# Attention and gated feed-forward on one core: the first load of k in four parts on two queues, and two one-row loads on a third

## The chip, the core and the metric

The kernel runs on one core of a Trainium2 chip. The metric is the device time in microseconds (us) of one execution; lower is better. The engines are named as in the profile: PE (TensorE, matrix products; PEld its weight loads), DVE (VectorE), ACT (ScalarE), POOL (GpSimd) and SP (SyncE, which here only issues transfers). Transfers between HBM and the on-chip memory are issued by SP, ACT or POOL, each on a queue of its own (q1, q10 and q0 in the profile), and are carried out by 16 DMA engines that all queues share.

## What is computed

Linear attention with cosine weights, then a gated feed-forward layer. Eight batches of eight heads, 576 tokens, head dimension 64.

```python
def _attn_ref(q, k, v):
    ...
    q_p = phi(q, cos_w, sin_w)          # relu(q) * cos, relu(q) * sin: 64 -> 128 features
    k_p = phi(k, cos_w, sin_w)
    kv = np.einsum('bhsf,bhsd->bhfd', k_p, v)
    z = np.sum(k_p, axis=2)
    num = np.einsum('bhsf,bhfd->bhsd', q_p, kv)
    den = np.einsum('bhsf,bhf->bhs', q_p, z)[..., None] + 1e-06
    return (num / den)
...
    rms = np.sqrt(np.mean(x * x, axis=-1, keepdims=True) + 1e-06)
    xn = x / rms * rms_g
    g = xn @ w_gate
    silu = g * (1.0 / (1.0 + np.exp(-g)))
    return (silu * (xn @ w_val) @ w_out)
```

The attention output of all heads side by side is x: 4608 tokens of 512. The feed-forward matrices are 512 x 1536 (two) and 1536 x 512. Inputs and output are float32.

## The kernel before

**The steady part.** The tokens are worked through in nine blocks of 512 (one for each batch, and one, block 8, of the last 64 tokens of the batches). In each block PE runs the gate and value products (half_mm, L556) in 12 steps, ACT and DVE turn their results into hT (L570, L571), and PE multiplies by the output matrix (out_mm, L574) in four more steps. Beside that, in slots written out by hand (the `at(block, step, where, ...)` calls), the attention of the next batch is prepared: loads, features of k and q (k_phi and q_phi, L292 on ACT and L294 on DVE), products of k and v (L387, L394), normalization (x_sq with a power on POOL at L520, x_norm at L527) and transposes through SP's queue (L346, L540).

**The beginning.** Batch 0 has no earlier block to hide behind, so its order is written out by hand. The loads are issued first:

- ACT's queue: the 2 KB vector rms_g (g4, L148). Ahead of it in ACT's program stands a table load (L62); behind it the activation that makes the table of sines and cosines, tab (L257), and then all of ACT's work on k.
- SP's queue: k of batch 0 in two loads (L150). In the tile for k, each of the 128 partitions holds nine consecutive tokens of one half of the heads: four head pairs, nine tokens, 64 values. The first load brings tokens 0 to 3 of every partition (512 KB in 512 pieces of 1 KB), the second tokens 4 to 8 (640 KB in 512 pieces of 1.25 KB).
- POOL's queue: half of q of batch 0 (load_q0, L135), v of batch 0 in two loads that convert it to bf16 (vv0, L213), the other half of q, then the feed-forward weights and the loads of batch 1 (L183, L110).

While they are under way PE runs ten matmuls on zeros (filler, L598). Then, for each token c of nine, `k_phi(V, 0, c, 0)` on DVE and `k_phi(A, 0, c, 1)` on ACT (the last one on DVE too) make the features, and z0_pe (L410) adds them up on PE; for c below 4, PE also spreads rms_g (g_spread, L233). k_phi of a token reads all four head pairs. Next kv0_pe (L430) multiplies features and v, two head pairs at a time; q's features are made and turned (q_tr_pe, L363), the sums are put in place (z0_turn, L421), kv0_pe does the other head pairs, and the chain through nd0_pe, x_sq, x_norm and x_tr_pe gives the first tokens of x, from which the dense feed-forward work of block 0 starts (unit_mm, L643).

**The late loads.** From batch 3 on (`wide`), load_kv lays k and v out with five consecutive tokens in a partition, and 576 tokens fill 115 partitions and a fifth of one more. For batch 7, the last of all, there is no next batch whose rows could fill that partition up, so a third load (L119) writes it: the last token, repeated five times, 40 pieces of 256 bytes. It is issued once for k, in step 0 of block 5, and once for v, in step 3 of block 5, by SP as all loads of load_kv at that point are. The tiles of the loads are a ring of five (`raw`).

Of the kernel before, what the change touches and what calls it, by code (L numbers as in the profile page):

```python
# [17 lines left out]
def kernel(  # L18
# [11 lines left out]
    nc = tc.nc  # L30
    B, H, S, D = q.shape
# [4 lines left out]
    HP = H // 2  # L36
    NC = S // 64
# [9 lines left out]
    V, A, G = nc.vector, nc.scalar, nc.gpsimd  # L47
# [22 lines left out]
    def kv_rows(src, b, hps):  # L70
        return src[b, 2 * hps[0] : 2 * hps[1], :, :].rearrange(
            "(hp hh) (s c) d -> (hh s) hp (c d)", hh=2, c=NC
        )

    def wide(b):
        return b > 2
# [4 lines left out]
    def kv_rows5(src, b, r0, r1):  # L81
        part = src[b, :, 0 : NC5 * (KP - 1), :].rearrange(
            "h (p c) d -> p h (c d)", c=NC5
        )[r0 : min(r1, KP - 1)]
        return bass.AP(part.tensor, part.offset, [[NC5 * D, r1 - r0]] + list(part.ap)[1:])
# [6 lines left out]
    def raw_tile(which, b):  # L92
        if (which, b) not in raw:
            t = ring.tile([P, H * NC5 * D], FP32, name="raw", tag="raw")
            raw[(which, b)] = t
        return raw[(which, b)]

    def raw_kv(which, b):
        t = raw_tile(which, b)
        if wide(b):  # L100
            return t[:, :].rearrange("p (h e) -> p h e", h=H)
        return t[:, 0 : HP * NC * D].rearrange("p (hp e) -> p hp e", hp=HP)
# [4 lines left out]
    def load_kv(which, b, hps=(0, HP), eng=nc.sync):  # L107
        src = k if which == "k" else v
        if not wide(b):
            return eng.dma_start(  # L110
                out=raw_kv(which, b)[:, hps[0] : hps[1], :], in_=kv_rows(src, b, hps)
            )
        last = KP if b < B - 1 else KP - 1
        for r0, r1 in ((0, KM), (KM, last)):
            eng.dma_start(
                out=raw_kv(which, b)[r0:r1, :, :], in_=kv_rows5(src, b, r0, r1)
            )
        if last < KP:
            eng.dma_start(  # L119
                out=raw_kv(which, b)[last:KP, :, :].rearrange("p h (c d) -> p h c d", d=D),  # L120
                in_=src[b, :, S - 1 : S, :].rearrange("h s d -> s h d").unsqueeze(2)
                .to_broadcast([1, H, NC5, D]),
            )
# [22 lines left out]

    g4 = one.tile([4, P], FP32, name="g4")
    nc.scalar.dma_start(out=g4[:, :], in_=moe_rms_g.rearrange("(t p) -> t p", p=P))  # L148
    for c0, c1 in ((0, 4), (4, NC)):
        nc.sync.dma_start(  # L150
            out=raw_kv("k", 0)[:, :, c0 * D : c1 * D],
            in_=kv_rows(k, 0, (0, HP))[:, :, c0 * D : c1 * D],
        )


# [67 lines left out]
    for i in range(3):  # L223
        m, e = math.frexp(left)
        part.append(math.ldexp(round(m * 256), e - 8))
        left -= part[i]
        G.memset(eps_rows[32 * i : 32 * i + 32, :], part[i] / 32)
    load_kv("k", 1, eng=G)
    load_w(wg, moe_w_gate, 8, NNT)

    def g_spread(bank, t):
# [12 lines left out]
        out=th[:, 0:NTAB], in0=fidx[:, :], scalar1=S - 1.0, scalar2=ang,  # L244
        op0=ALU.min, op1=ALU.mult,
    )
    for c0, c1, i0, less in ((0, 9, 0, 576.0), (13, 14, 13, 64.0), (19, NTAB, 13, 64.0)):
        V.tensor_scalar(
            out=th[64:128, c0:c1], in0=fidx[64:128, i0 : i0 + c1 - c0],
# [4 lines left out]
        out=th[:, NTAB : 2 * NTAB], in0=th[:, 0:NTAB], scalar1=math.pi / 2.0,  # L254
# [4 lines left out]
        out=sel[:, :, :], in_=ident[0:4, 0:4].unsqueeze(2).to_broadcast([4, NDT, P])  # L259
# [437 lines left out]
    x_sq(0, 1)  # L697
    load_q(1, eng=G)
    load_kv("v", 1, eng=G)
    x_norm(0, 0, (0, HALF))  # L700
    x_norm(0, 0, (HALF, DM))
# [63 lines left out]
    for j in range(4):  # L765
# [3 lines left out]
        if j < 2:  # L769
            at(0, 10 + j, "pe", q_tr_pe, 1, j, bank)  # L770
            at(0, 10 + j, "pre", q_tr_evac, V, 1, j, bank)
    at(0, 8, "post", load_kv, "k", 2, (0, HP), G)
    at(0, 9, "post", v_cast, G, 1, (0, 2))
    at(0, 10, "pre", v_cast, V, 1, (2, 4))
# [184 lines left out]
```

## Time and profile before

| what | value |
| --- | --- |
| median of 3 runs | 323.27 us (323.22 to 323.35) |
| the profiled execution | 322.91 us |
| its span, first to last instruction | 321.1 us |
| PE busy | 313.6 us (98% of the span) |
| DVE, ACT, POOL busy | 185.4, 165.8, 40.5 us |
| issue of the two k loads on SP | 0.72 to 1.73 us |
| issue of rms_g on ACT | 0.75 to 1.31 us |
| first step on k, ACT and DVE | 5.04 and 5.06 us |
| first v load: issue on POOL, down | 3.02, 9.83 us |
| kv0_pe starts | 9.87 us |
| dense work of block 0 starts (L643) | 17.3 us |
| L119 on SP (k, v) | at 195.02 for 0.80 us, at 201.80 for 1.00 us |

The span is what the profile covers; the execution's own time is 1.8 us longer. Times within the profile count from the span's start. A line such as `9.87 0.71 PE psG L430 x36` in the chain of waits means: from 9.87 us on, 0.71 us of the chain were 36 matmuls of line 430 that write psG. In the timeline the bracket at the end of a line gives the idle time of that engine just before, and what ended it. In a table of windows each engine has its busy time and, in brackets, its number of instructions; the last three columns are the granted PE clock (1.00 is full), the mean share of the 16 DMA engines that was busy, and GB/s. That share adds up the times of packets and can pass 1.

### The profile page before, as it was taken

Reading aid. Unit: us, or ns where it says so; the run is one execution under the profiler, and the core shown is the slowest. Engines: PE = TensorE matmul, PEld = TensorE weight load, DVE = VectorE, ACT = ScalarE, POOL = GpSimd, SP = SyncE. Lnnn points to the kernel's source line nnn. Section 1 sums busy time; section 2 is a strip of 40 time slices with the busy share of each in tenths; the row PEclk is TensorE's granted clock in tenths of the full one; section 3 lists DMA queues with packets and bytes.
Section 4 is the critical chain, followed back from the end, with each engine's and each line's share of the span. In section 5 each row is a group of like instructions: output and inputs, shape, how many; then the busy total and the mean of one; then the engine's idle time right before and its main releaser. Section 6 shows DMA issues by size and latency. Waiting matters only on the chain.

```text
span 321.1 us, 6023 instructions
## 1 busy us (share of the span) xinstructions
PE 313.6 (98%) x2274; PEld 162.4 (51%) x2310; DVE 185.4 (58%) x382; ACT 165.8 (52%) x322; POOL 40.5 (13%) x79
## 2 busy tenths in 40 slices
PE   7999999999999999999999999999999999999996
PEld 2689564544454445444544445544544444444444
DVE  7976977668457773777457644781676034204410
ACT  5766756754574466554744575446543233223321
POOL 9771211002001100010001100100011000000000
PEclk9999999999999999999999999999999999999999
DMA  7999999788999999999799959995522500041002
GB/s 232 239 270 269 282 329 227 201 183 190 223 226 211 187 263 187 221 247 182 162 186 230 197 163 200 197 217 163 99 59 41 116 33 0 0 102 31 1 35 98
DMA packets 80092, 53.76 MB, mean 167 GB/s; under 512 B 52235, under 2 KB 74047, under 8 KB 80063
## 3 DMA queue, kind: packets, MB, share of 16 engines
q1 hardware_dynamic: 73110, 41.25, 62.1%
q0 software_dynamic: 6944, 12.13, 15.5%
q8 instruction: 18, 0.29, 0.4%
q14 instruction: 12, 0.09, 0.1%
q10 hardware_dynamic: 8, 0.00, 0.0%
HBM read 37.83 MB, written 9.44 MB: 147 GB/s over the span
## 4 chain that ended last, share of the span: by engine, by line
PE 94%; DMA 2%; DVE 1%; issue 1%; POOL 1%; ACT 0%; POOLq 0%; ACTq 0%
PE psC L574 27%; PE psV L556 27%; PE psG L556 26%; PE psV L643 2%; PE psA L449 2%; DMA vv<-in_v_dram 2%; PE psG L574 2%; PE psG L643 2%; PE psA L387 2%; PE psA L394 1%; PE psA L474 0%; PE psV L363 0%; PE psG L430 0%; PE psC L546 0%; POOL raw L135 0%
## 5 line engine op out<-in xcount | busy, mean ns | idle before, releaser
L571 DVE TENSOR_TENSOR hT<-psV,sg 128x512 bf16<-128x512 f32 x99 | 68.2, 689 | 96.5 <-PE psV L556 64.1
L556 PE MATMUL psV<-xnT,wv 128*128 128x512 bf16 x344 | 89.6, 379 | 0.7 <-issue 0.2
L570 ACT ACTIVATE sg<-psG 128x512 f32<-128x512 f32 x99 | 58.6, 592 | 60.8 <-PE psG L556 52.7
L556 PE MATMUL psG<-xnT,wg 128*128 128x512 bf16 x337 | 88.5, 379 | 0.7 <-issue 0.2
L574 PE MATMUL psC<-wo,hT 128*128 128x512 bf16 (+1 forms) x400 | 88.4, 376 | 0.4
L574 PEld LDWEIGHTS <-hT 128*128 128x128 bf16 x456 | 43.1, 98 | 47.7
L556 PEld LDWEIGHTS <-wv 128*128 128x128 bf16 x400 | 39.0, 98 | 46.8
L556 PEld LDWEIGHTS <-wg 128*128 128x128 bf16 x400 | 37.0, 98 | 39.9 <-DVE xnT L288 0.2
L520 POOL TENSOR_TENSOR rs<-ms,mhalf 128x1 f32<-128x1 f32 x36 | 20.5, 570 | 193.9 <-ACT scr L515 193.7
L286 ACT COPY osb<-psC 128x512 f32<-128x512 f32 x32 | 18.7, 585 | 49.9 <-PE psC L574 46.1
L515 ACT ACTIVATE scr<-xt 128x513 bf16<-128x513 f32 x36 | 22.8, 635 | 23.3 <-DVE xt L499 22.3
L527 DVE SCALAR_TENSOR_TENSOR xn<-xt,rs,gb 128x512 bf16<-128x512 f32 (+1 forms) x37 | 26.9, 730 | 9.9 <-POOL rs L520 9.9
L292 ACT ACTIVATE kp<-raw,tab 128x256 bf16<-128x256 f32 (+2 forms) x51 | 28.8, 607 | 2.4 <-DMA raw<-in_k_dram 2.4
L499 DVE TENSOR_TENSOR xt<-psA,rec 128x512 f32<-128x512 f32 x36 | 24.9, 691 | 1.2
L292 ACT ACTIVATE qp<-raw,tab 128x512 bf16<-128x512 f32 (+1 forms) x36 | 23.3, 666 | 1.2 <-DMA raw<-in_q_dram 1.1
L294 DVE TENSOR_SCALAR kp<-raw,tab 128x256 bf16<-128x256 f32 (+2 forms) x53 | 20.1, 428 | 0.5 <-DMA raw<-in_k_dram 0.5
L294 DVE TENSOR_SCALAR qp<-raw,tab 128x512 bf16<-128x512 f32 (+1 forms) x34 | 15.3, 463 | 4.7 <-DMA raw<-in_q_dram 4.7
L449 PEld LDWEIGHTS <-qpT 128*128 128x128 bf16 x224 | 10.6, 97 | 6.6
L556 PE MATMUL psV<-xnT_tail,wv 128*128 128x512 bf16 x48 | 12.3, 379 | 0.1
L556 PE MATMUL psG<-xnT_tail,wg 128*128 128x512 bf16 x46 | 12.0, 379 | 0.1
L288 DVE CAST vv<-raw 116x1280 bf16<-116x1280 f32 (+1 forms) x13 | 11.1, 857 | 1.3 <-DMA raw<-in_v_dram 1.3
L449 PE MATMUL psA<-kvzs,qpT 128*128 128x65 bf16 x224 | 11.4, 193 | 0.0
(102 smaller groups left out, 177.7 us busy)
## 6 DMA issues: line engine op xcount, KB each, us to landing
out_dram<-osb SPq DMA_DIRECT2D x27, 256.0 KB, 2.3
raw<-in_q_dram SPq DMA_DIRECT2D x6, 1024.0 KB, 9.1
raw<-in_k_dram SPq DMA_DIRECT2D x5, 1120.0 KB, 8.8
raw<-in_v_dram SPq DMA_DIRECT2D x5, 1120.0 KB, 9.4
raw<-in_k_dram POOLq DMA_DIRECT2D x2, 1152.0 KB, 19.2
raw<-in_v_dram POOLq DMA_DIRECT2D x2, 1152.0 KB, 15.7
out_dram<-osb SPq DMA_DIRECT2D x17, 128.0 KB, 2.6
wg<-in_moe_w_gate_dram POOLq DMA_DIRECT2D x3, 512.0 KB, 13.8
```

Source lines behind the costliest of these rows:

```text
L286: A.copy(out=o, in_=i)
L292: A.activation(out=out_ap, in_=in_ap, func=AF.Relu, scale=scale)
L294: eng.tensor_scalar(out=out_ap, in0=in_ap, scalar1=scale, scalar2=0.0, op0=ALU.mult, op1=ALU.max)
L449: nc.tensor.matmul(heads[:, g, hp, :], lhsT=qpT[:, h, j * P : (j + 1) * P], rhs=kvzs[b][:, g, hp * E : (hp + 1) * E], start=True, stop=True,)
L499: V.tensor_tensor(out=xt[:, 0:DM].rearrange("p (hp g d) -> p g hp d", g=2, d=D), in0=heads[:, :, :, 0:D], in1=rec[:, :, :].unsqueeze(3).to ...
L515: A.activation(out=scr[:, :], in_=xt[:, 0 : DM + 1], func=AF.Square, scale=1.0 / math.sqrt(DM), accum_out=ms[:, :],)
L520: G.tensor_tensor(out=rs[:, :], in0=ms[:, :], in1=mhalf[:, :], op=ALU.pow)
L527: V.scalar_tensor_tensor(out=xn_of[(b, j)][:, c], in0=x_of[(b, j)][:, c], scalar=rs_of[(b, j)][:, :], in1=gb[:, c], op0=ALU.mult, op1=ALU. ...
L556: nc.tensor.matmul(bank[:, cols[0] : cols[1]], lhsT=w[:, t, n * P : (n + 1) * P], rhs=x[:, t, cols[0] : cols[1]], start=(t == 0), stop=(t ...
L570: A.activation(out=sg[:, :], in_=g[:, 0:TB], func=AF.Silu)
L571: V.tensor_tensor(out=hT[:, n, :], in0=v[:, 0:TB], in1=sg[:, :], op=ALU.mult)
L574: nc.tensor.matmul(bank[:, 0 : cols[1] - cols[0]], lhsT=hT[:, n, j * P : (j + 1) * P], rhs=wo[:, n, cols[0] : cols[1]], start=(n == 0), st ...
```

## The change

k of batch 0 comes in four loads in place of two, each of 256 pieces: the first four tokens of every partition in two loads on SP's queue (head pairs 0 and 1, then 2 and 3), the other five tokens in two loads on ACT's queue, split in the same way. ACT issues its two right behind rms_g. And the one-row load of L119 is always issued by GpSimd, whatever queue load_kv was given; in this program it occurs twice, for k and v of batch 7.

```diff
@@ -116,7 +116,7 @@
                 out=raw_kv(which, b)[r0:r1, :, :], in_=kv_rows5(src, b, r0, r1)
             )
         if last < KP:
-            eng.dma_start(
+            G.dma_start(
                 out=raw_kv(which, b)[last:KP, :, :].rearrange("p h (c d) -> p h c d", d=D),
                 in_=src[b, :, S - 1 : S, :].rearrange("h s d -> s h d").unsqueeze(2)
                 .to_broadcast([1, H, NC5, D]),
@@ -146,10 +146,13 @@
 
     g4 = one.tile([4, P], FP32, name="g4")
     nc.scalar.dma_start(out=g4[:, :], in_=moe_rms_g.rearrange("(t p) -> t p", p=P))
-    for c0, c1 in ((0, 4), (4, NC)):
-        nc.sync.dma_start(
-            out=raw_kv("k", 0)[:, :, c0 * D : c1 * D],
-            in_=kv_rows(k, 0, (0, HP))[:, :, c0 * D : c1 * D],
+    for eng, hps, c0, c1 in (
+        (nc.sync, (0, 2), 0, 4), (nc.sync, (2, HP), 0, 4),
+        (nc.scalar, (0, 2), 4, NC), (nc.scalar, (2, HP), 4, NC),
+    ):
+        eng.dma_start(
+            out=raw_kv("k", 0)[:, hps[0] : hps[1], c0 * D : c1 * D],
+            in_=kv_rows(k, 0, hps)[:, :, c0 * D : c1 * D],
         )
```

## The prediction, made before the changed kernel was run

> **What bounds the kernel now.** I read the page first, then PE's busy time by stages, then the chain of waits of the first 35 us, then the timeline of the first 10 us, and last the traffic of the DMA queues in small windows.
>
> ```profile
> span 321.1 us, 6023 instructions
> ```
>
> ```profile
> 0.00:17.46 17.46, 14.75 (x197) 8.42 (x200) 14.63 (x42) 12.01 (x27) 14.40 (x38) 1.00 1.01 233
> 17.46:60.00 42.54, 42.23 (x470) 28.74 (x474) 33.48 (x72) 28.56 (x58) 10.07 (x15) 1.00 1.13 278
> ...
> 190.00:222.00 32.00, 31.79 (x208) 15.68 (x211) 19.55 (x39) 16.98 (x33) 2.19 (x4) 1.00 1.02 195
> ```
>
> The first column after the length of a window is PE's busy time. From 17.46 us on PE is busy for all but about 1% of each window (42.23 of 42.54, 31.79 of 32.00). So nothing after 17.46 us can be won by an earlier transfer; an edit matters only if it moves the moment at which that dense stretch begins, and then it moves the end by as much. The change touches the first 7 us and two small loads near 195 and 202 us.
>
> The chain of waits says what sets the start of the dense stretch:
>
> ```profile
> 2.01 1.01 POOL raw L135
> 3.02 6.81 DMA vv<-in_v_dram
> 9.82 0.04 issue
> 9.87 0.71 PE psG L430 x36
> ```
>
> It is not k but v: kv0_pe (L430) waits for the first v load on GpSimd's queue, down at 9.83. k comes close behind, as the timeline shows:
>
> ```profile
> 0.72 1.01 SPq L150 DMA_DIRECT2D raw<-in_k_dram  x2
> 0.75 0.56 ACTq L148 DMA_DIRECT2D g<-in_moe_rms_g_dram  x1
> 2.43 0.24 ACT L257 ACTIVATE tab<-th 128x40 f32<-128x40 f32 x1 [0.43 <-DVE th L253]
> 5.06 3.79 DVE L294 TENSOR_SCALAR kp<-raw,tab 128x256 bf16<-128x256 f32 x10 [0.55 <-DMA raw<-in_k_dram]
> 8.91 0.39 PE L410 MATMUL psV<-kp,ones 64*128 64x512 bf16 x1
> ```
>
> The first tokens of k are down at 5.04; DVE and ACT work through k without a pause, and PE's sums of k (L410) end at 8.91 + 0.39 = 9.30. Then PE idles 0.57 until v. **The slack of k is thus about 0.53 us**: a k that is later by less costs nothing, and an earlier k alone gains nothing.
>
> **The change, part by part.** All sums are against the profiled execution (322.91 us; span 321.1, 1.8 around it); the median of the runs shown, 323.27, lies 0.36 above, and I give results on that scale.
>
> *Issues.* SP still issues two loads (0.46 and 0.49 us in the trace, 1.01 together); only their size falls. ACT gets two more behind g's, at 1.31 (0.75 + 0.56). At 0.5 to 0.56 each, by the rows above, ACT's sequencer is free again at about 2.35. What is queued behind them is the table activation at 2.43, which waits for DVE until 2.40, so it is hidden; were it 0.5 late, nobody would notice, since ACT and DVE use the table first at 5.04. Cover: 2.4 us. The first DVE and ACT instructions on k now wait for two loads in place of one: 0 to 0.06 us (the gap between SP's two issues), taken as 0.05, inside the slack.
>
> *The tiny loads.* L119 leaves SP (0.80 and 1.00 us of issue there, at 195.0 and 201.8) and goes to POOL, where the nearest rows are 0.73 to 1.08 us per issue. POOL's instruction in that stretch is the power at L520, 0.55 us each; POOL stands idle 15.55 us before the one at 199.85 and 3.83 before the one at 204.23, so 2 x 1 us fits. Were the cover gone, 1 us on POOL would delay the normalization of a token group used only from 222 us on. Their data are wanted by DVE at 213.4 (k) and 214.6 (v); POOL's loads land 6.6 to 20.9 us after issue, so k's, issued near 195, would at the slow end be down near 216. But those 20 us are 1 MB loads in the opening traffic; these carry 10 KB each. SP's transposes behind them come up to 1.8 us earlier, which PE, busy 31.79 of 32.00, cannot use. I take 0, with a bound of 0 to +0.3.
>
> *The transfers themselves.* This is the disputed part: where do the bytes of the two ACT loads come in the 16 engines' order? What the trace shows of their traffic, in windows (last two columns: share of the 16 engines, GB/s):
>
> ```profile
> 1.75:2.25 0.50, 0.50 (x3) 0.15 (x1) 0.43 (x5) 0.25 (x1) 0.50 (x7) 1.00 0.65 72
> 2.25:2.75 0.50, 0.50 (x2) 0.15 (x1) 0.50 (x3) 0.24 (x1) 0.50 (x1) 1.00 0.55 111
> 2.75:3.25 0.50, 0.50 (x2) 0.15 (x1) 0.47 (x2) 0.00 (x0) 0.50 (x2) 1.00 0.87 246
> 3.25:3.75 0.50, 0.50 (x3) 0.19 (x2) 0.47 (x2) 0.00 (x0) 0.50 (x2) 1.00 1.07 379
> ```
>
> Two things: k begins at about 1.8, some 1.1 after SP's issue, and crawls for 1.4 us before it flows at 380 to 390 GB/s. And how two queues share is seen where both have work, here k (q1) against GpSimd's queue (q0) from 5.75 to 6.25, and a transpose (q1) behind a v load (q0) from 48.7 to 49.0:
>
> ```profile
> q0 software_dynamic: 38, 0.16, 91.6%
> q1 hardware_dynamic: 33, 0.03, 19.9%
> ```
>
> ```profile
> q1 hardware_dynamic: 153, 0.04, 57.0%
> q0 software_dynamic: 18, 0.06, 49.4%
> ```
>
> The second fence is the telling one: 153 packets of one queue beside 18 of the other, although q0 had been alone until 48.5 and the transpose had been issued at 45.88. Packet about, the counts would be near equal. It looks as if each engine ends what one queue has handed it and then takes the other. By that, the ACT loads, whose first packets come at about 1.31 + 1.1 = 2.4, stand behind SP's (from 1.8) and ahead of GpSimd's (its first 7 packets fall between 5.25 and 5.75): the same order of bytes as now. First tokens 5.04 + 0.05, the others at 6.74 (L150's second issue at 1.24 plus the 5.5 us that it took to land), v at 9.83. **Sum: 0.05 inside a slack of 0.53, so 0; 323.3 us.**
>
> The Trainium skill's page "DMA: Bandwidth & Descriptors", section "Queues, rings and completion order", says otherwise: an engine goes round its queues and changes at each packet. The 153 against 18 speaks against it, but those were two different kinds of queue; by that rule the result is the first rival.
>
> **The rivals.**
>
> *First tokens late (slower).* SP's and ACT's queues alternate packet by packet from 2.4 on. The bytes moved by then: 0.5 x 72 + 0.15 x 111 = 53 KB; 471 of the 524 KB of the first tokens remain, and with 1,024 of each 2,304 bytes they need 1,060 KB of traffic. 39 + 123 KB pass until 3.25, the remaining 898 KB at 385 GB/s take 2.33: 5.58. The same sum for now (309 KB after 3.25) gives 4.05, so the first tokens are 1.5 late. That exceeds the slack of 0.53 by 1.0: PE's sums end at 10.8 in place of 9.30, and kv0_pe starts 1.0 later. 324.3. It decides from a delay of 0.53 on; with half the alternation (0.75 late) it costs 0.2. For it: engines stand 35 to 45% idle in the crawl, just when ACT's packets arrive, and an idle engine will take them. Against: the 153 to 18.
>
> *The crawl is filled (faster).* If ACT's queue uses the idle share from 2.4 to 3.25, up to 385 x 0.85 - 39 - 123 = 165 KB move earlier, 0.43 us; k ends 0.43 earlier, and since q0 set in near 5.5 only as q1 ran out, v would be down at 9.40 and kv0_pe starts 0.43 sooner. 322.8; PE's own end at 9.30 bounds the gain at 0.57. For it: the idle share. Against: the crawl is seen with the descriptors of two loads already issued, so more issues may not lift it. The Trainium skill's page "Perfetto Trace Analysis", section "DMA Optimizations", advises splitting where engines are idle; that is this rival, and the trace has the idle share only until 3.25.
>
> *The other tokens late (slower).* GpSimd's queue gets in ahead of ACT's second load. Its first q load (512 KB, 1.4 us at 385) then delays the tokens that DVE needs at 6.76; less the slack, +0.9: 324.2. Against: q0's first packets come near 5.5, three us after ACT's.
>
> **How the numbers follow.** A measurement here tells about 0.2% (0.65 us) from no change. Order kept 0.48 (323.1 to 323.5); first tokens late 0.27 (323.4 to 324.4, about two thirds of it beyond 323.9); crawl filled 0.18 (322.7 to 323.1; only if k's first tokens also gain does it pass 322.6); others late 0.07 (324.2). Slower by over 0.2%: 0.18 + 0.05 = 0.23; faster 0.07 (a third of the filled crawl); the rest, 0.70, within. The range leaves out the far end of each rival: 322.7 to 324.3.
>
> **What would show it.** Right: in the chain DMA of v still ends near 9.8, DVE's first step on k starts within 0.5 of 5.06, PE's idle before L430 stays 0.3 to 0.6. First rival: DVE's first k step after 5.6, and L430 no longer released by v but by k's features. Second: GB/s above 111 in 2.25 to 2.75 and v down before 9.6. Third: a pause of DVE and ACT in mid k. The tiny loads: any PE gap above 0.1 us between 190 and 250 us that is not there now would prove me wrong on them.

## The result, and the profile after

The changed kernel took 324.07 us (median of 22 executions, 322.88 to 326.29), the kernel before 323.26 us beside it (22 executions, 322.79 to 324.15): 1.0034 times as long, 95% interval 1.0018 to 1.005. It is slower, by 0.8 us in the median. The forecast was 323.3 us and no change that can be measured; the time lies in the range (322.7 to 324.3), but there is a change clear of the noise. The ratios here and below leave out executions more than 1.5% slower than the fastest of their kernel: one of the kernel before (414.29 us, beside e9 to e12), one of e11 (1890.86 us) and two of e14 (328.24 and 328.34 us).

The spread says more than the median: 11 of the 22 executions are slower than the slowest of the kernel before, and the other 11 have a median of 323.47. So there are two things to explain: a small loss, which the better half shows too, and a larger one that half of the executions have. The profiled execution (323.37 us) is one of the better half.

The first line of its page:

```profile
span 321.6 us, 6068 instructions
```

The timeline of the profile after, first 10 us (start, length, engine, line, operation, then the idle time and what ended it). It answers to the timeline shown of before, three lines further down in the code (L294 there is L297 here, L410 is L413, L430 is L433):

```profile
1.35 0.93 ACTq L153 DMA_DIRECT2D raw<-in_k_dram  x2
...
2.43 0.24 ACT L260 ACTIVATE tab<-th 128x40 f32<-128x40 f32 x1 [0.42 <-DVE th L256]
...
5.22 1.70 ACT L295 ACTIVATE kp<-raw,tab 128x256 bf16<-128x256 f32 x4 [2.56 <-DMA raw<-in_k_dram]
5.24 1.63 DVE L297 TENSOR_SCALAR kp<-raw,tab 128x256 bf16<-128x256 f32 x4 [0.68 <-DMA raw<-in_k_dram]
7.88 1.71 ACT L295 ACTIVATE kp<-raw,tab 128x256 bf16<-128x256 f32 x4 [0.96 <-DMA raw<-in_k_dram]
7.90 1.96 DVE L297 TENSOR_SCALAR kp<-raw,tab 128x256 bf16<-128x256 f32 x6 [1.02 <-DMA raw<-in_k_dram]
```

The first features start 0.18 later than before (5.24 for 5.06). Then both engines stop after four tokens and wait 1 us for the other five: this pause in mid k is not in the kernel before, where DVE goes through all ten steps from 5.06 to 8.85.

The chain of waits of the profile after:

```profile
1.25 3.87 DMA raw<-in_k_dram
...
5.22 0.52 ACT kp L295
...
9.64 0.37 PE psC L413
...
10.04 0.24 PE psC L413
...
10.30 0.53 PE psG L433 x36
...
17.48 0.22 PE psG L601
17.69 0.90 PE psG L646 x16
```

The load of v, which stood in the chain of before up to 9.82, is gone from it: v is down at 9.84 as before, but k's sums on PE now end after it, and kv0_pe (L433) starts at 10.12 where it started at 9.87. The first long run of dense work, at 17.46 before, comes at 17.69. From there on PE has no gap over 0.13 us, so these 0.23 us reach the end whole; the two profiled executions differ by 0.46, the rest being within what repeated runs of one kernel differ by.

How late k is, is not to be read from the time at which most of it is there. The trace has, for each load, when each of the 16 DMA engines reported its part done; an instruction that reads the load waits for the last of the sixteen (ACT and DVE go on at 7.88 and 7.90 us, just behind the 7.80 of the last). Median engine and last engine, in us:

| load of k | before | after |
| --- | --- | --- |
| first four tokens, last of their loads | 4.51, 4.95 | 4.66, 5.11 |
| other five tokens, last of their loads | 6.31, 6.74 | 6.07, **7.80** |

Fifteen engines have the last load done by 6.53, earlier than before. The sixteenth takes 1.27 us more. What it does meanwhile, in the traffic of the DMA queues of the profile after from 6.60 to 7.60 (queue: packets, MB, share of 16 engines):

```profile
q0 software_dynamic: 126, 0.26, 99.3%
q10 hardware_dynamic: 8, 0.01, 2.7%
```

The last eight packets of ACT's queue (q10) run beside GpSimd's work (q0). The trace does not name a packet's engine, but each engine ends its part of a load with a packet of 4 bytes (36 on ACT's queue: four for rms_g, sixteen for each load of k), and of the last load's sixteen fifteen have started by 6.066 and one starts at 7.265: the pieces between are the sixteenth's. Single pieces of 1,280 bytes start at 6.035, 6.242, 6.467, 6.679 and 6.916, some 0.21 us apart, though a piece takes 0.06: between two of them fits one packet of 4 KB of GpSimd's queue (0.16 to 0.22 us each in that stretch). The last six pieces, from 6.916 on, follow each other 0.05 to 0.07 us apart. So on this engine the two queues take turns packet by packet for a while. By these rows that is about half of its 1.27 us (an estimate: four spaces of 0.16 us beyond a piece's own 0.06); by the rest it was behind already. The profile of e16 below shows the turns one by one.

### The profile page after: what moved, and what is told of

Its sections match the earlier page's. It is cut to its first block, busy times and chain, and to the rows that moved or that the text cites. A ratio compares the mean times of both kernels' runs of the same rounds, so it can differ in the third digit from the quotient of the medians.

```text
span 321.6 us, 6068 instructions
## 1 busy us (share of the span) xinstructions
PE 317.2 (99%) x2310; PEld 162.7 (51%) x2310; DVE 185.1 (58%) x382; ACT 165.9 (52%) x322; POOL 41.9 (13%) x81
## 4 chain that ended last, share of the span: by engine, by line
PE 94%; DMA 3%; ACT 1%; SPq 0%; DVE 0%; issue 0%; POOL 0%; ACTq 0%
PE psG L559 27%; PE psV L559 27%; PE psC L577 26%; PE psV L646 2%; PE psA L452 2%; PE psG L577 2%; PE psG L646 2%; PE psA L390 2%; DMA xnT_tail<-xn 1%; DMA raw<-in_k_dram 1%; PE psC L413 1%; PE psA L397 1%; ACT qp L295 0%; PE psA L477 0%; PE psV L366 0%; PE psC L549 0%
## 5 line engine op out<-in xcount | busy, mean ns | idle before, releaser
L559 PE MATMUL psG<-xnT,wg 128*128 128x512 bf16 x352 | 90.3, 379 | 0.0
L297 DVE TENSOR_SCALAR kp<-raw,tab 128x256 bf16<-128x256 f32 (+2 forms) x53 | 19.9, 423 | 1.7 <-DMA raw<-in_k_dram 1.7
L297 DVE TENSOR_SCALAR qp<-raw,tab 128x512 bf16<-128x512 f32 (+1 forms) x34 | 15.2, 460 | 4.2 <-DMA raw<-in_q_dram 4.2
```

Of the source, the lines that this page charges most:

```text
L297: eng.tensor_scalar(out=out_ap, in0=in_ap, scalar1=scale, scalar2=0.0, op0=ALU.mult, op1=ALU.max)
L559: nc.tensor.matmul(bank[:, cols[0] : cols[1]], lhsT=w[:, t, n * P : (n + 1) * P], rhs=x[:, t, cols[0] : cols[1]], start=(t == 0), stop=(t ...
```

## The experiments

Two causes of a late k were open (the one-row loads, the loads of k), and for the loads of k which property of the four: a second queue (theory A), their smaller size (256 pieces in place of 512, each piece as long as before; theory C, and in narrower forms D, E and G), or their number (theory H). Theory B is that the one-row loads cost the time. Letters in the quoted expectations are those of the theories as they stood at the time; where one needs a word it is given. The ratios are to the kernel before, run beside each experiment.

### Which half of the change

**e1: the four loads alone.** The changed kernel, with the one-row load back on the queue it had:

```diff
         if last < KP:
-            G.dma_start(
+            eng.dma_start(
```

> The four loads of k as in the change; the one-row loads stay on SP. Theory A (the last tokens of k come late because their tail on ACT's queue takes turns with GpSimd's packets): as the changed kernel, 323.9 to 324.5 us, single executions up to 326, the second half of k's features starting near 7.9 us. Theory B (the one-row loads on GpSimd's queue cost the time, by disturbing PE late): as before, 323.3 us.

324.41 us (323.35 to 326.66, 12 executions), ratio 1.0043 [1.0024, 1.0062]. The whole loss is there without the one-row loads. In its profile (325.19 us) the last load of k is down on the median engine at 6.12 and on the last at 7.99, and DVE pauses for 1.26 us.

**e2: the one-row loads alone.** The kernel before with only the other edit:

```diff
         if last < KP:
-            eng.dma_start(
+            G.dma_start(
```

> Only the one-row loads move to GpSimd's queue; k of batch 0 as before. Theory A: 323.2 to 323.4 us, no execution above 324.5. Theory B: 324 us, single executions up to 326.

323.28 us (322.89 to 323.69), ratio 1.0003 [0.9995, 1.0012]: nothing. In its windows PE is busy without a break where the issues were moved:

```profile
190.00:256.00 66.00, 66.00 (x445) 32.34 (x444) 36.87 (x74) 33.44 (x66) 4.94 (x9) 1.00 0.67 138
```

Theory B falls.

### Second queue, size of a load, or number of loads

**e4: two loads as before, the second on ACT's queue.**

```diff
-    for c0, c1 in ((0, 4), (4, NC)):
-        nc.sync.dma_start(
+    for eng, c0, c1 in ((nc.sync, 0, 4), (nc.scalar, 4, NC)):
+        eng.dma_start(
```

> k in two loads of 512 pieces as before, the first on SP's queue and the second on ACT's; one-row loads on SP. Theory A: as the changed kernel, 323.9 to 324.5 us, the second half of k's features starting near 7.5 to 8 us. Theory C: 323.3 us.

322.88 us (322.49 to 324.05, 12 executions), ratio 1.0002 [0.9991, 1.0014]. The second load's parts come in between 6.01 and 6.48, no engine late, and ACT, in its timeline, goes through all its tokens at one go:

```profile
4.79 3.42 ACT L293 ACTIVATE kp<-raw,tab 128x256 bf16<-128x256 f32 x8 [2.13 <-DMA raw<-in_k_dram]
```

A second queue by itself is harmless, with GpSimd's beside it too. Theory A, which I held until then, falls.

**e3: the four loads all on SP's queue.**

```diff
-        (nc.scalar, (0, 2), 4, NC), (nc.scalar, (2, HP), 4, NC),
+        (nc.sync, (0, 2), 4, NC), (nc.sync, (2, HP), 4, NC),
```

(the one-row load as before, here and in e5, e6, e9 and e10).

> k in the same four loads of 256 pieces, all four on SP's queue; one-row loads on SP. Theory A (the second queue is what hurts): 323.2 to 323.5 us, the second half of k's features starting near 6.8 us. Theory C (the smaller loads hurt by themselves): 324 us or more, features late as in the changed kernel.

327.43 us (326.3 to 329.18, 6 executions), ratio 1.0138 [1.0116, 1.016]: the worst of all, on one queue. Its first tokens are down early, at 4.27, but the parts of the third load come in from 4.84 to 8.63 and those of the fourth from 5.74 to 9.48, and DVE waits for them, as its timeline says:

```profile
4.40 1.68 DVE L297 TENSOR_SCALAR kp<-raw,tab 128x256 bf16<-128x256 f32 x4
9.58 1.79 DVE L297 TENSOR_SCALAR kp<-raw,tab 128x256 bf16<-128x256 f32 x6 [3.50 <-DMA raw<-in_k_dram]
```

Here many engines fall behind, not one. So the queue of ACT isn't the cause; if anything it softens it.

**e5: three loads, ACT's in one.** **e6: three loads, SP's in one.**

```diff
-        (nc.scalar, (0, 2), 4, NC), (nc.scalar, (2, HP), 4, NC),
+        (nc.scalar, (0, HP), 4, NC),
```

```diff
-        (nc.sync, (0, 2), 0, 4), (nc.sync, (2, HP), 0, 4),
+        (nc.sync, (0, HP), 0, 4),
```

> First tokens in two loads of 256 pieces on SP's queue, the others in one load of 512 on ACT's; one-row loads on SP. Theory D (it is the last load's small size that lets an engine fall behind: between ACT's two small loads it turns to GpSimd's queue and then takes turns with it): the other tokens land within 6.7 us on all engines, clock at 0.999 or more in all executions, 322.6 to 323.4 us, first tokens earlier than before (under 4.9 us). Theory E (small loads at the head of SP's queue are what spreads the engines): the last engine lands after 7.3 us and 324 us or more.

> First tokens in one load of 512 pieces on SP's queue, the others in two of 256 on ACT's; one-row loads on SP. Theory D: the last engine lands at 7.3 us or later, 323.9 to 324.6 us, single executions up to 326 with a mean clock of 0.989 to 0.995. Theory E: all engines within 6.7 us and 322.8 to 323.4 us.

e5: 323.60 us (12 executions), 1.0014 [1.0002, 1.0025]; e6: 323.81 us (11 executions), 1.0012 [1.0003, 1.002]. The last load is down at 6.26 and 6.72 on the last engine, so neither of the profiled executions has the late one. What is left is about a third of the loss. Theory D asked for a late engine in e6, theory E for one in e5, and the times of both missed what either had given for the even case: neither holds as it stood.

**e9: two loads of 256 pieces** (of 2,304 bytes: all nine tokens of two head pairs), on SP. **e10: four loads of 512 pieces** (512 bytes three times, 768 once: tokens 0 and 1, 2 and 3, 4 and 5, 6 to 8), on SP and ACT. The features' first tokens need both loads in e9 and only one in e10.

```diff
-        (nc.sync, (0, 2), 0, 4), (nc.sync, (2, HP), 0, 4),
-        (nc.scalar, (0, 2), 4, NC), (nc.scalar, (2, HP), 4, NC),
+        (nc.sync, (0, 2), 0, NC), (nc.sync, (2, HP), 0, NC),
```

```diff
-        (nc.sync, (0, 2), 0, 4), (nc.sync, (2, HP), 0, 4),
-        (nc.scalar, (0, 2), 4, NC), (nc.scalar, (2, HP), 4, NC),
+        (nc.sync, (0, HP), 0, 2), (nc.sync, (0, HP), 2, 4),
+        (nc.scalar, (0, HP), 4, 6), (nc.scalar, (0, HP), 6, NC),
```

> k in only two loads, each of 256 pieces of 2304 bytes (head pairs 0 and 1, then 2 and 3, all nine tokens), both on SP's queue; one-row loads on SP. All of k's features wait for both, so the time says little; the landings decide. Theory G (an engine falls behind when its share of a load is small, 16 pieces): the last engine lands 0.8 us or more after the median engine. Theory H (it is the number of loads under way, four against two): the 16 engines land within 0.6 us of each other, by about 6.7 us, as in the kernel before.

> k in four loads of 512 pieces each (all head pairs; tokens 0-1 and 2-3 on SP's queue, 4-5 and 6-8 on ACT's, pieces of 512 to 768 bytes); one-row loads on SP. Theory G: no engine falls behind, all within 0.6 us of the median, 323.2 to 323.7 us. Theory H: the last engine lands 0.8 us or more after the median in the last load, 324 us or more, some executions with a mean clock under 0.997.

e9: its parts come in from 3.88 to 4.31 and from 5.44 to 5.81, all within 0.4 us, and all of k is down 0.9 us earlier than in the kernel before. (It is slower all the same, 325.1 us, 1.0082 [1.0054, 1.0109]: no token can start before 5.81, and in its profile the first sum starts at 6.48 and full clock is granted only at 13.70. What that has to do with each other is the last question below.) e10: 326.19 us, 1.0071 [1.0031, 1.0111]; the last load is down on the median engine at 6.58, on the last three at 8.15, 9.27 and 9.77. Its DVE and ACT, in the timeline:

```profile
9.80 1.27 DVE L297 TENSOR_SCALAR kp<-raw,tab 128x256 bf16<-128x256 f32 x4 [3.46 <-DMA raw<-in_k_dram]
...
9.80 0.91 ACT L295 ACTIVATE kp<-raw,tab 128x256 bf16<-128x256 f32 x2 [3.11 <-DMA raw<-in_k_dram]
```

So neither the number of pieces in a load nor their size decides: 256 pieces in two loads are even, 512 in four are not. Nor does the number of pieces in all, which is 1,024 in the kernel before and in the changed one. Put in one table, the last load of k in the profiled executions:

| loads of k | run | median engine, us | last engine, us |
| --- | --- | --- | --- |
| 2 on SP | before | 6.31 | 6.74 |
| 2 on SP, by head pairs | e9 | 5.67 | 5.81 |
| 1 on SP, 1 on ACT | e4 | 6.21 | 6.48 |
| 3 | e5, e6 | 6.10, 6.35 | 6.26, 6.72 |
| 4 on SP and ACT | after, e1 | 6.07, 6.12 | 7.80, 7.99 |
| 4 on SP and ACT, again | e12, e16 (below) | 6.17, 6.21 | 6.41, 10.09 |
| 4 on SP and ACT, of 512 | e10 | 6.58 | 9.77 |
| 4 on SP | e3 | 7.81 | 9.48 |

With two queues the median engine stays between 6.06 and 6.58, whatever the number of loads. The last one does not. One profile says little, since the engine is not late each time; but over all profiles, those below included, it is more than 1 us behind the median in seven of ten with four loads (after, e1, e3, e7, e10, e14, e16; 0.25 to 0.86 in e8, e11 and e12), and never more than 0.5 in six with two (before, e2, e4, e9, e13, e15). Theory H, the number of loads under way, is what is left; that small loads as such do not do it rests on e9's one profile. Why an engine falls behind when four are under way, no run shows.

### GpSimd's packets and the late engine

**e8: GpSimd's loads 0.85 us later.** Its small fills are moved ahead of its loads; the first is issued at 2.81 in place of 1.96 (I had reckoned with 1.7 us). The edit is shortened here: the fills of eps_rows and eps_ones come ahead of the loads too.

```diff
+    G.memset(vv[:, :, :, D:E], 1.0)
+    G.memset(vv5[:, :, :, D:E], 1.0)
     vv0 = one.tile([P, HP, NC * D], BF16, name="vv0")
     load_q0(0, G)
...
-    G.memset(vv[:, :, :, D:E], 1.0)
-    G.memset(vv5[:, :, :, D:E], 1.0)
```

> The changed kernel with four groups of small fills that GpSimd otherwise does after its loads put ahead of them, so that its queue starts some 1.7 us later. Theory D: without GpSimd's packets beside it the last engine of k's last load lands by 6.7 us, the second half of k's features starts by 6.8; v lands later, so PE waits for v and the time is 1 to 2 us above before. If ACT's last load is late by itself: still 7.5 us or later.

323.69 us (322.74 to 326.25, 8 executions), 1.0027 [1.0002, 1.0052]. The last engine is at 6.97, the fifteenth at 6.26; the lag is still there and shorter. But the later issue did not move what it was to move: GpSimd's first data packet starts at 5.24 us here and at 5.26 in the changed kernel. The interval holds the changed kernel's own ratio too, so this run settles nothing.

**e11: GpSimd's loads far later.** A large fill ahead of them delays the first issue to 4.55.

```diff
+    hT = one.tile([P, NNT, TB], BF16, name="hT")
+    G.memset(hT[:, 0:6, :], 0.0)
     vv0 = one.tile([P, HP, NC * D], BF16, name="vv0")
...
-    hT = one.tile([P, NNT, TB], BF16, name="hT")
```

> The changed kernel with a fill of half of hT on GpSimd ahead of its loads, so that its first packets come 2 us or more later, after k. Theory D' (the last engine's last pieces are late because they take turns with GpSimd's packets): the last engine of k's last load lands by 6.7 us; v comes 2 us later and the time is 1.5 to 3 us above before. If the engine is late without GpSimd: 7.3 us or later.

Ratio 1.011 [1.0078, 1.0142], from three executions of 326.0 to 327.2 us. The profiled execution is the fourth, of 1890.86 us, in which PE is slow throughout: its ten matmuls on zeros take 13.14 us where they take 3.90 in the kernel before. So the profile tells nothing of where the three others lose some 3.6 us (the first load of v is down at 10.27 in it, 0.44 later than before, which is not enough). Of the transfers it tells this: GpSimd's first data packet starts at 6.22, and the last load of k is down at 6.06 on the median engine and at 6.59 on the last. With few of GpSimd's packets beside it, no engine was late in this one profile. That fits a late tail that comes of an engine behind and of a queue with long packets to take turns with; that it needs both isn't shown, as in e12 no engine was late (6.41) with all of GpSimd's packets there.

### The clock

Half of the changed kernel's executions are some 1.7 us worse than the others (medians 325.13 and 323.47), more than a k that is 1 us late explains. Their mean granted clock tells them apart: ten of the eleven slower ones have 0.989 to 0.995 (the eleventh, 326.29 us, has 0.999), all of the eleven faster ones 0.999 or more. Of the 105 executions of the kernel before beside the experiments (without that of 414.29 us), one has less than 0.997 (324.37 us, 0.994). The profiled execution of e1 (325.19 us, 0.995) is like the slower ones, and it shows PE at half clock for 3.41 us, from 9.49 to 12.91, in its windows (the third column from the right is the granted clock):

```profile
6.08:9.49 3.41, 3.11 (x26) 1.41 (x25) 2.15 (x7) 2.27 (x7) 3.33 (x8) 1.00 1.11 244
9.49:12.91 3.42, 3.42 (x53) 2.60 (x53) 2.73 (x8) 2.35 (x6) 1.37 (x4) 0.50 1.15 279
```

Its 36 matmuls of L433 take 1.22 us where the same 36 take 0.71 in the kernel before. One such window is 1.7 us of work lost and 0.005 of the mean clock over 322 us, an estimate from these rows that fits the distance of the two halves. Theory P: PE's idle time at the start leads to the half clock. Rival Q: it goes with the disturbed transfers in some other way.

**e7: work for PE in its wait.** Seven matmuls on zeros between the sums of k, in the changed kernel:

```diff
             g_spread(psC[0], c)
+        if 3 <= c < 8:
+            filler(3 if c == 3 else 1, psV[0])
```

> The changed kernel with matmuls on zeros in PE's program where it waits for the later tokens of k: three after token 3, one after each of tokens 4 to 7. Theory F (the slow executions are those in which PE, short of work while the later tokens are late, is granted half the clock for some 3.4 us): mean clock 0.999 or more in all executions, none above 324.7, median 323.4 to 324.2 us. If the clock has another cause: as the changed kernel, half of the executions at 0.989 to 0.995 and 324.5 to 326.3.

325.02 us (324.56 to 328.82, 12 executions), 1.0074 [1.005, 1.0097]: worse. Nine of the 12 executions have a mean clock of 0.999 or more and took 324.56 to 325.68, so it seems that the added matmuls cost some 1 us themselves; three have 0.990 to 0.995. The profiled execution lost its time before them: one engine was late already in the second load (6.04, the others by 4.98), so PE idled 1.87 us before its first sum, and the half clock followed. It doesn't tell the two theories apart.

**e12: the changed kernel again.**

> The changed kernel once more, for a second profile of it. If its slow executions come from an engine that lags in k's loads and the half clock that follows: an execution of 324.5 us or more shows k's last landing at 7.9 us or later and a stretch of some 3.4 us with matmuls at twice their length before 15 us; one of 323.9 or less shows the last landing under 7.9 and no such stretch.

324.73 us (323.47 to 327.15, 7 executions), 1.0047 [1.0017, 1.0076]. The profiled execution (324.41 us) is not what I expected: the last load of k is down at 6.41, on time, and yet it is 1.5 us slower than the profiled one of the kernel before. Only the first tokens are 0.38 late (5.33), PE idles 0.94 us ahead of its first sum, and then this, in its windows:

```profile
4.75:8.16 3.41, 2.47 (x20) 0.88 (x17) 2.70 (x7) 2.72 (x7) 3.41 (x5) 1.00 1.06 309
8.16:11.58 3.42, 3.42 (x41) 1.65 (x41) 2.63 (x9) 2.63 (x7) 2.75 (x9) 0.50 1.15 269
```

A window in which PE was busy 2.47 of 3.41 us is followed by one at half clock.

**e13: an idle PE without touching a transfer.** The kernel before, with six matmuls on zeros at the start in place of ten. **e14: the changed kernel with twelve.**

```diff
-    filler(10, psC[1])
+    filler(6, psC[1])
```

```diff
-    filler(10, psC[1])
+    filler(12, psC[1])
```

> The kernel before with six matmuls on zeros at the start of PE's program in place of ten; no transfer is touched. They take 0.39 us each, so PE ends them near 3.5 in place of 5.07 and idles about 2.1 us before its first sum of k, where it idled 0.58. Theory P, that an idle PE is what leads to the half clock: k's features, v and the start of kv0_pe stay as they are (9.87), but at least a third of the executions shows a mean clock below 0.997, these are 1.2 to 3.5 us slower, and the median is 323.8 to 325.5. Rival Q, that the half clock goes with the disturbed transfers and not with PE: no execution below 0.997, median 323.0 to 323.5.

> The changed kernel with twelve matmuls on zeros in place of ten, so that PE works until about 5.85 and hardly idles before its first sum of k, which it starts at about 5.8 anyway; the pause in the middle of k stays. If PE's idle time before z0_pe is what leads to the half clock (theory P), at most 2 in 12 executions are below 0.997 and the median falls to 323.3 to 323.7. If the pause in the middle of k is enough, about half are still low and the median is 323.9 to 324.6. By rival Q nothing changes either: about half are low.

e13: 324.82 us (323.56 to 326.23, 12 executions), 1.0042 [1.0025, 1.0059]. k and v come as in the kernel before (the last parts at 4.88, 6.68 and 9.84), and the kernel loses as much as the changed one does. Its profile (323.67 us), in PE's timeline; a pair of sums, one line each in psC and psV, takes 0.37 to 0.39 at full clock and 0.60 to 0.63 at half:

```profile
5.53 0.37 PE L410 MATMUL psC<-kp,ones 64*128 64x512 bf16 x1 [1.61 <-ACT kp L292]
...
6.72 0.39 PE L410 MATMUL psV<-kp,ones 64*128 64x512 bf16 x1
...
7.30 0.60 PE L410 MATMUL psC<-kp,ones 64*128 64x512 bf16 x1
7.31 0.61 PE L410 MATMUL psV<-kp,ones 64*128 64x512 bf16 x1
```

That is theory P's result in the time, and Q falls as far as it said that only a disturbed transfer brings the half clock. But only 3 of 12 executions had a mean clock below 0.997, fewer than P asked for, and these were the faster ones (323.56 to 323.75; the others 324.74 to 326.23). e14: 324.02 us, 1.0018 [0.9995, 1.0041], 4 of 12 below 0.997 (326.32 to 328.34 us): between the two answers, and no finding by itself. In its profile (326.32 us) PE idles 0.50 before its first sum, as little as in the kernel before, but the last engine is down at 8.93, PE waits 1.39 us in mid k, and a half-clock window from 10.69 follows. There the wait was in mid k.

**e15: e13's kernel once more; e16: the changed kernel a third time.** No edit.

> The kernel before with six matmuls on zeros once more, for a profile of one of its executions with a mean clock of 1.0 (9 of 12, 324.7 to 326.2 us, slower than the three with a window at half clock, 323.6 to 323.8). Theory P: the clock changes on a grid of 3.41 us, and in these executions full clock is granted first one or two windows later than in the kernel before (there at 4.38), so that k's sums and kv0_pe run at half clock although the mean counts only from the first grant: first grant after 8 us, 36 matmuls of L430 in about 1.2 us. Rival: the first grant is as early as before and the time is lost elsewhere (DMA).

> The changed kernel a third time, for where its clock windows lie. By theory P the window granted depends on where the grid of 3.41 us falls on PE's idle stretch (0.4 us before z0_pe, then the pause in mid k): either full clock from about 5 to 7 us on and 323.2 to 324.0 us, or a window of 3.41 us at half clock between 7 and 13 us and 324.4 to 326.3. k's last landing on at least one engine is 1 us or more behind the median engine.

e15 (324.78 us) is one of e13's slower kind, with a mean clock of 0.999. In PE's timeline all of k's sums are at half clock, and the products behind them start 1.70 us later than before:

```profile
5.58 0.58 PE L410 MATMUL psC<-kp,ones 64*128 64x512 bf16 x1 [1.67 <-ACT kp L292]
...
11.15 0.63 PE L410 MATMUL psC<-kp,ones 64*128 64x512 bf16 x1
...
11.57 0.88 PE L430 MATMUL psG<-vv,kp 64*128 64x64 bf16 x36
```

The trace records the first grant of full clock at 11.97 us; in the kernel before it is at 4.38. The mean clock of a run counts only from that first grant on, so it hides this kind; counting executions by it was a mistake of mine, which this run settles. The 36 products take 0.88 us and not the 1.2 expected, since the grant comes among them. P holds for this kernel in the wider form that e15's expectation gave it.

e16 (326.48 us) fits neither case of its expectation for the clock and has both troubles: the first grant at 13.77, and the last load of k down at 10.09 on one engine (the other fifteen by 7.04). DVE's timeline, and the traffic from 7.20 to 10.20:

```profile
5.50 1.63 DVE L297 TENSOR_SCALAR kp<-raw,tab 128x256 bf16<-128x256 f32 x4 [0.94 <-DMA raw<-in_k_dram]
10.19 2.09 DVE L297 TENSOR_SCALAR kp<-raw,tab 128x256 bf16<-128x256 f32 x6 [3.05 <-DMA raw<-in_k_dram]
```

```profile
q0 software_dynamic: 525, 0.64, 116.5%
q10 hardware_dynamic: 9, 0.01, 1.0%
```

Nine packets of k in 3 us: from 7.88 on eight of its pieces start 0.207 to 0.239 us apart, and at the end of each but the last one packet of 4 KB of GpSimd's queue begins (7.882 and 7.934, 8.089 and 8.141, and so on to 9.136 and 9.203). These turns make up about 1.15 of the 3.05 us by which the engine is last; from 6.57 to 7.88 no piece of k runs on any engine, and what held this one there isn't shown. The dense work starts at 20.68 where it started at 17.31 in the kernel before: 3.37 us, of a difference of 3.57 us between the two executions.

All profiles together: the windows of the clock are 3.41 us long, and where they lie differs from one execution to the next of nearly the same start (first grant at 3.85, 4.38, 4.59, 5.63, 5.92 us in e13, before, e6, e2, e8). Waits of PE of 0.86 to 1.93 us ahead of or among the sums of k were followed by half clock, or by a first grant after 11 us, in each profile that has one (e3, e7, e9, e10, e12, e13, e14, e15); before's 0.58 was followed by neither. But waits and busy time alone aren't the rule. A window of e2 with PE busy 2.41 of 3.41 us, a wait for v of 1.00 in it, was not followed by half clock, and one of e1 with 3.11 busy and no wait over 0.29 was. In e16 PE waits only 0.57 us ahead of its first sum, as long as in the kernel before, and yet full clock comes at 13.77. So it is shown that less work of PE at the start brings the half clock with no transfer touched (e13, e15), and e12 and e14 fit a wait as its cause in the changed kernel. What brought it in e1 and e16, which have the late engine and no such wait ahead of the sums, stays open.

## Why the prediction was wrong, step by step

- **What bounds the kernel: right.** From 17.5 us on nothing changed, and what moved the start of the dense work moved the end (0.23 in the profile after, 3.37 of 3.57 in e16).
- **Issues: right.** ACT's two issues took 0.93 us (1.35 to 2.28; I had said free at about 2.35), and the table activation stands at 2.43 as before.
- **The tiny loads: right.** 0 us, by e2.
- **The transfers themselves: this is the step that failed.** "By that, the ACT loads ... stand behind SP's ... and ahead of GpSimd's: the same order of bytes as now ... the others at 6.74 ... Sum: 0.05 inside a slack of 0.53, so 0". It holds on fifteen engines of sixteen (6.53 at the latest in the profile after). It does not hold on the last, 7.80 in place of 6.74, and k's readers wait for that one. I treated the 16 engines as one pipe with one order. (ACT's first packets of k came at 3.36 and not at 2.4, GpSimd's at 5.26: the order of the starts was right.) The 153 packets beside 18, "the telling one", was misread with it: over 16 engines a count cannot tell an engine that serves one queue after the other from engines that are done with one of them, and in the 0.2 us before, 48.5 to 48.7, it is 16 beside 18. Single pieces 0.21 us apart show the turn-taking where an engine has both. That is the rule of the Trainium skill's page "DMA: Bandwidth & Descriptors", section "Queues, rings and completion order", which I had weighed and set aside; the trace agrees with it on the engine that is behind (pieces 0.207 to 0.239 us apart in e16). The page's packets are 9 to 17 descriptors long as a rule; in e16 the turn came after each single piece of 1,280 bytes. Why that engine had pieces of k left when GpSimd's packets came is the part that stays open.
- **The slack: somewhat small, and it explains the smaller loss.** The last pair of sums starts at 9.91 after, at 8.91 before: 1.0 late, about as late as the load (7.80 for 6.74). kv0_pe follows 0.21 behind it after, so before it could have started at 9.12 and waited for v until 9.87: a slack of 0.75, where I took 0.53 from the modelled ends of the sums. 1.0 less 0.75 is the 0.25 by which kv0_pe is later.
- **A term that was not in the sum: the clock.** The prediction worked at full clock throughout. Ten of the 22 executions have a mean clock of 0.995 or less, and they make the larger loss. In e12, on time with its last load and with first tokens 0.38 us late, PE's longer wait was followed by 3.41 us at half clock, and the execution is 1.5 us slower. e13 and e15 have the half clock with no transfer touched.
- **The rivals.** "The other tokens late" was the right kind, with the sign for it that I had named (a pause of DVE and ACT in mid k) and a chance of 0.07; its mechanism, GpSimd's queue getting ahead of ACT's second load, holds on one engine. That its 324.2 is close to the median of 324.07 is luck: the mechanism costs 0.23 us in the profile after, and the median lies between two halves at 323.47 and 325.13 that the clock sets apart. "First tokens late" did not come about: 5.11 for 4.95, not 1.5 us. "The crawl is filled" came half true: the traffic from 2.25 to 2.75 rose from 111 to 276 GB/s, as the window below of the profile after shows, but nothing came of it, since the first tokens and v are not earlier. e4, with ACT's queue and loads of 512 pieces, has 88 GB/s there, so it was not the second queue that filled it; e3 and e9, with loads of 256 pieces on SP's queue alone, have 268 and 281.

```profile
2.25:2.75 0.50, 0.50 (x2) 0.15 (x1) 0.50 (x3) 0.24 (x1) 0.50 (x1) 1.00 0.84 276
```

**Still open:** why an engine falls behind with four loads of k under way and not with two; why it is mostly one engine with two queues and most of them with one (e3); and what work of PE within a window is enough to keep the clock, with it what took the clock in e1 and e16. That the half clock can be taken away by keeping PE busy wasn't shown (e7 and e14 don't decide it); that less work of PE at the start brings it on was (e13, e15).

## What to carry to other kernels

A load is there when the slowest of its 16 engines has written its part: before splitting a load that a chain waits for, and after, look at the last landing and not at the bulk, in several profiles, for the late engine is not late every time. Few loads in flight kept the engines even here (with two the last was within 0.5 us of the median, with four up to 3.9 behind it), and an engine that is behind shares its time with whatever large transfers were queued next. Where PE waits at the start of a kernel, a few tenths of a microsecond more can be followed by a window at half clock (0.94 us in e12, 0.58 in the kernel before); such a kernel should be judged over many executions. Their mean clock tells of a window at half clock behind the first grant, and of none ahead of it (e15).

## What the runs showed of the hardware that was not expected

- An engine with work of two queues can alternate at each packet: in e16 eight pieces of 1,280 bytes (0.06 us each) 0.21 us apart, with one 4 KB packet of the other queue between each two.
- Four loads on one queue spread the landings of one load over 3.8 us (4.84 to 8.63 in e3); two spread them over 0.4 (e9) to 0.7 (before).
- When GpSimd's loads are issued isn't when their packets start: issued from 1.96 us on they start at 5.26 (after), from 2.81 on at 5.24 (e8), from 4.55 on at 6.22 (e11).
- The clock is granted in windows of 3.41 us whose place differs between executions; a PE at full clock fell back in the window after one with a wait of 0.94 us (e12). The Trainium skill's page "TensorE: Matmul & The Clock Gate", section "What's actually happening", has such windows that run freely, of about 3.4 us, and half clock after an idle one; the traces agree on the length and on the running freely (3.41 us; first grants from 3.85 to 5.92), but here less than an idle window was enough.
- A run's mean granted clock counts from the first grant on: e15 shows 0.999 with its first 12 us at half clock.
